# Sums over keys moved in front of the values, their additions moved behind the scores, in a fused attention and MLP kernel

## Chip, cores and metric

The kernel runs on one core of one Trainium2 chip. The metric is device time in microseconds (us) of one execution. The kernel before the change takes 1482.98 us, the median of 3 runs (1481.69 to 1483.19).

## What is computed

Attention with normalised queries and keys (8 batches, 12 heads, 448 positions, 64 features per head), followed by a two-layer MLP with the activation h - tanh(h), all in float32:

```python
q_n, k_n = rmsnorm(q, g_q), rmsnorm(k, g_k)
scores = 1/sqrt(64) * q_n @ k_n.T          # (8, 12, 448, 448)
attn = exp(scores - max); attn = attn / (sum over keys + 1e-9)
x = (attn @ v), heads side by side          # (3584, 768)
h = x @ w_in                                # (3584, 2048)
out = (h - tanh(h)) @ w_out                 # (3584, 768)
```

The weights arrive as float64 and are turned into float32 words on the chip.

## The kernel before

The work on attention is cut into 48 steps, one for each of 8 batches and 6 pairs of heads (`NP` = 6). The steps are pipelined by hand: the program of one slot `s` does the last part of step s, the scores of step s+1, transposes of step s+2, the normalising of step s+3 and the loads of step s+4. The order in which the code emits instructions is the order in each engine's queue.

The parts of a step, with their lines:

- `squares` and `norm` (L344 to L361): ScalarE squares q and k, VectorE sums the squares (L357) and scales (L359), GpSimd takes the power -1/2 (L360). `norm_q` (L363) then multiplies q on VectorE (L366), which waits for that power. `turn` (L372) transposes k and q on TensorE (L377, L381); ScalarE copies them out.
- `scores(s, half)` (L391): four matmuls (L401) with 64 rows each, two heads at a time in the two row halves of the array, give the transposed scores (keys on partitions, queries along the free axis). ScalarE takes exp straight from PSUM into the tile `p` (L406). A step has two halves, so two tiles `p` of 112 x 2 x 2 x 448.
- `add(s)` (L410): from a certain step on VectorE adds the four key chunks of `p` into one tile `sum` of 112 x 2 x 448 (one L418 and two L420). Below that step there is no addition and `sums[s]` is empty.
- `totals(s, bank)` (L435): matmuls with a matrix of ones (L443), 32 columns wide, four side by side in the array's column strips, sum over the keys. With a `sum` tile these are 4 matmuls, without one 16. VectorE takes the reciprocal from PSUM into `rs` (L448).
- `values(s, bank)` (L422): 16 matmuls (L429) of the values, also in four column strips of 32.
- `divide(s, bank)` (L450): four VectorE multiplications of the values by `rs` (L456); for the last three head pairs of a batch four more operations, on GpSimd (L469 to L472), prepare the factors of the MLP.

The profile counts two matmul instructions and two weight loads for each float32 matmul of the code.

The MLP of batch b runs during the attention of batch b+1. It is a stream (`mlp`, L687) of matmuls of 128 x 128 x 224 at L510, in a form that computes seven products instead of eight blocks (`ORDER` = 1, 5, 6, 2, 3, 7, 4). `run(ns)` (L698) takes matmuls off the stream until their planned time is used up. From slot 12 on a gap is 14 matmuls of L510, and a slot has four gaps; three slots do the first layer (`hidden`, seven products of 6 matmuls for each of four `j`), three the second (`project`, seven products of 8 matmuls for each of three `j`). The MLP of batch 0 runs in slots 6 to 11; there the second layer is written plainly (`project_first`, L675), and the weights are still being converted: ScalarE at L71 and L72, VectorE at L78, L79 and L82, GpSimd at L90, each piece behind its load.

Two pools of PSUM banks set how far TensorE can run ahead. The MLP has three banks in rotation: products 1, 5 and 6 open a bank, 2, 3 and 7 go on in those of 1, 5 and 6 once these have been read, and 4 opens the next. The readers of the first layer are L564 (ScalarE) for 1, L566 for 5, L568 for 6, L546 and L547 for 2, L576 for 3, L572 and L573 for 7, L580 for 4; all but L564 and the tanh of L546 are VectorE's. Attention has five banks `sc` in rotation: scores, transposes, totals and values take them in the order in which they are emitted.

Other tiles that matter here: `sum` and `rs` have one buffer each, `p` has three.

Slots 0 to 5 are `first_slot`; from slot 6 on it is `slot` (L743), which holds the order that is changed.

Of the kernel before, what the change touches and what calls it, by code (L numbers as in the profile page):

```python
# [92 lines left out]
def bounded_path(tc, ctx, q, k, v, moe_w_in, moe_w_out, out, g_col, ident, ones, neg_half):  # L93
# [21 lines left out]
    NP = H // 2  # L115
# [38 lines left out]
    def load(s, names):  # L154
        b, hp = steps[s]
        for name in names:
            src = {"q": q, "k": k, "v": v}[name]
            bufs = 3 if name == "v" else 2
            pair = src[b, 2 * hp : 2 * hp + 2].rearrange("h (p c) d -> p h c d", c=NCH)
            if name == "k":  # L160
                t = nat.tile([CP, NCH, 2, D], F32, name="k_nat", bufs=bufs)
                for h in range(2):
                    nc.sync.dma_start(out=t[:, :, h, :], in_=pair[:, h])
            else:
                t = nat.tile([CP, 2, NCH, D], F32, name=f"{name}_nat", bufs=bufs)
                nc.sync.dma_start(
                    out=t.rearrange("p h c d -> p h (c d)"), in_=pair.rearrange("p h c d -> p h (c d)")
                )
            loaded[name, s] = t
# [174 lines left out]
    def squares(s):  # L344
        n = nat.tile([CP, NCH, 2, D], F32, name="n", bufs=1)
        sq = nat.tile([CP, 2 * NCH, D], F32, name="sq", bufs=1), n.rearrange("p c h d -> p (c h) d")
        normed[s] = sq, n
        for i, name in ((1, "q"), (0, "k")):
            nc.scalar.activation(sq[i], loaded[name, s].rearrange("p a b d -> p (a b) d"), AF.Square)

    def norm(s):

        sq, n = normed[s]
        rr = small.tile([CP, 2, 2 * NCH], F32, name="rr", bufs=3)
        for group in ((1,), (0,)) if s < NP else ((0, 1),):
            for i in group:
                nc.vector.reduce_sum(rr[:, i], sq[i], axis=AX.X)  # L357
            r = rr[:, group[0] : group[-1] + 1].rearrange("p i r -> p (i r)")
            nc.vector.tensor_scalar(out=r, in0=r, scalar1=1.0 / D, scalar2=1e-6, op0=ALU.mult, op1=ALU.add)  # L359
            nc.gpsimd.tensor_tensor(out=r, in0=r, in1=neg_half[:, : r.shape[1]], op=ALU.pow)  # L360
        normed[s] = rr, n  # L361
# [10 lines left out]
    def turn(s, tk, tq):  # L372

        rr, n = normed.pop(s)
        kn = loaded.pop(("k", s))
        for c in range(NCH):
            nc.tensor.transpose(tk[:, c * CP : (c + 1) * CP], kn[:, c].rearrange("p h d -> p (h d)"), ident[:CP, :CP])  # L377
        kT = qkp.tile([P, S], F32, name="kT")
        nc.scalar.mul(kT, tk[:, :S], g_col)
        for c in range(NCH):  # L380
            nc.tensor.transpose(  # L381
                tq[:, c * CP : (c + 1) * CP], n[:, c].rearrange("p h d -> p (h d)"), ident[:CP, :CP]
            )
        qT = qkp.tile([P, S], F32, name="qT")
        nc.scalar.copy(out=qT, in_=tq[:, :S])
        turned[s] = rr, kT, qT

    def sc_bank():
        return ps_s.tile([P, 512], F32, name="sc")

    def scores(s, half):  # L391

        rr, kT, qT = turned[s]
        p = probs[s, half] = pp.tile([CP, 2, NCH // 2, S], F32, name="p")
        for i in range(NCH // 2):
            c = half * (NCH // 2) + i
            tiles = []
            for h in range(2):
                r = slice(h * D, (h + 1) * D)
                sc = sc_bank()  # L400
                nc.tensor.matmul(  # L401
                    sc[:CP, :S], lhsT=kT[r, c * CP : (c + 1) * CP], rhs=qT[r, :], start=True, stop=True
                )
                tiles.append(sc)
            for h in range(2):
                nc.scalar.activation(  # L406
                    p[:, h, i, :], tiles[h][:CP, :S], AF.Exp, scale=rr[:, 0, 2 * c + h : 2 * c + h + 1]
                )

    def add(s):  # L410

        if s < NP + NP // 2:
            sums[s] = []
            return
        t = sp.tile([CP, 2, S], F32, name="sum")
        sums[s] = [t]
        parts = [probs[s, c // 2][:, :, c % 2, :] for c in range(NCH)]
        nc.vector.tensor_tensor(out=t, in0=parts[0], in1=parts[1], op=ALU.add)  # L418
        for part in parts[2:]:
            nc.vector.tensor_tensor(out=t, in0=t, in1=part, op=ALU.add)  # L420

    def values(s, av):  # L422
        v_nat = loaded.pop(("v", s))
        for c in range(NCH):
            p = probs[s, c // 2]
            for m in range(2):
                for h in range(2):
                    r = (2 * m + h) * BL
                    nc.tensor.matmul(  # L429
                        av[r : r + BL, :S], lhsT=v_nat[:, h, c, m * BL : (m + 1) * BL], rhs=p[:, h, c % 2, :],  # L430
                        start=(c == 0), stop=(c == NCH - 1),
                    )
        return av

    def totals(s, dn):  # L435

        t = sums.pop(s)
        parts = t if t else [probs[s, c // 2][:, :, c % 2, :] for c in range(NCH)]
        for i, p in enumerate(parts):
            for n in range(2):  # L440
                for h in range(2):
                    r = (2 * n + h) * BL
                    nc.tensor.matmul(  # L443
                        dn[r : r + BL, :HS], lhsT=ones[:CP, :BL], rhs=p[:, h, n * HS : (n + 1) * HS],
                        start=(i == 0), stop=(i == len(parts) - 1),
                    )
        rs = whole[s] = sp.tile([P, HS], F32, name="rs")
        nc.vector.reciprocal(rs, dn[:, :HS])  # L448

    def divide(s, av):  # L450
        b, hp = steps[s]
        rs = whole.pop(s)
        x = xT[b, hp] = xp.tile([P, S], F32, name="xT")
        for n in range(2):
            for m in range(2):
                nc.vector.tensor_tensor(  # L456
                    out=x[m * D : (m + 1) * D, n * HS : (n + 1) * HS],
                    in0=av[m * D : (m + 1) * D, n * HS : (n + 1) * HS], in1=rs[n * D : (n + 1) * D], op=ALU.mult,
                )
        del probs[s, 0], probs[s, 1]  # L460
        if hp < HC:
            return
        c = hp - HC
        if c == 0:
            tt[b] = tp.tile([P, 3, HC, HS], F32, name="tt", bufs=1)
        eng = nc.vector if b == 0 and c == HC - 1 else nc.gpsimd
        x11, x12, x21, x22 = (xT[b, r][:, n : n + HS] for r in (c, hp) for n in (0, HS))
        t1, t2, t4 = (tt[b][:, i, c] for i in range(3))
        eng.tensor_tensor(out=t1, in0=x12, in1=x11, op=ALU.subtract)  # L469
        eng.tensor_tensor(out=t2, in0=x22, in1=t1, op=ALU.subtract)  # L470
        eng.tensor_tensor(out=x12, in0=x22, in1=x12, op=ALU.subtract)
        eng.tensor_tensor(out=t4, in0=x21, in1=t2, op=ALU.subtract)  # L472
# [225 lines left out]
    def run(ns):  # L698

        spent[1] += ns  # L700
        while spent[0] + 1.0 < spent[1]:
            took = next(stream, None)
            if took is None:
                return
            spent[0] += took
# [4 lines left out]
    def gap_ns(s):  # L710

        if s < 2 * NP:
            return H_NS / 12 if s % NP < 3 else 4 * S / ENGINE_NS * CD * CF / 12
        return (H_NS + O_NS) / (4 * NP)

    def has(s):
        return 0 <= s < NS
# [24 lines left out]

    def slot(s):  # L743
        gap = gap_ns(s)
        totals(s, sc_bank())
        if has(s + 1):
            scores(s + 1, 0)
        if has(s + 2):
            load(s + 2, "v")
        run(gap)  # L750
        if has(s + 2):
            turn(s + 2, sc_bank(), sc_bank())
        if has(s + 3):
            squares(s + 3)
        if has(s + 4):
            load(s + 4, "kq")
        run(gap)
        divide(s, values(s, sc_bank()))
        if has(s + 1):
            scores(s + 1, 1)  # L760
        if has(s + 3):
            norm(s + 3)
        run(gap)
        if has(s + 1):
            add(s + 1)
        if has(s + 3):
            norm_q(s + 3)
        run(gap)
# [10 lines left out]
    for s in range(NP, NS):  # L779
        slot(s)  # L780
# [319 lines left out]
```

## Time and profile before

| engine | busy us | share of the span |
|---|---|---|
| TensorE matmuls (PE) | 1442.1 | 97% |
| TensorE weight loads (PEld) | 1142.9 | 77% |
| VectorE (DVE) | 791.8 | 54% |
| ScalarE (ACT) | 469.6 | 32% |
| GpSimd (POOL) | 469.0 | 32% |

The span of the profiled execution is 1479.9 us. The page's row of slices shows TensorE at 90% or more in all but the first and the last few slices, VectorE at 80% or more in the first six (about 220 us, the conversion of the weights) and mostly at 30 to 60% after that. The granted TensorE clock is at 0.9 or more throughout.

How to read the lines: a group has its line, engine, operation, output and inputs, shapes and count, then its busy time and mean. A line of the timeline has the start in us from the span's start, the duration, the engine, the operation and its count, and in square brackets the idle time ahead of it with what ended it. The end of a matmul is modelled: consecutive matmuls overlap in the record, and distances between starts are what counts.

### The profile page before, as it was taken

What the parts mean: (1) busy time and instruction counts of PE and PEld (TensorE: products, weight loads), DVE (VectorE), ACT (ScalarE), POOL (GpSimd) and SP (SyncE); (2) the same over time, 40 slices, a digit from 0 to 9 for tenths busy, and PEclk for the clock granted to TensorE, in tenths of its full rate; (3) what the DMA queues carried; (4) which work ended last, traced back from release to release, by engine and by line L of the source; (5) the groups of instructions that cost most, each with busy time, mean ns of one, the idle gap of its engine ahead of it and who ended that gap; (6) DMA issues with size and microseconds to landing.
All of it is one profiled execution on the core that took longest, in us unless ns stands there. A gap on an engine that the chain in (4) does not pass through costs nothing.

```text
span 1479.9 us, 22097 instructions
## 1 busy us (share of the span) xinstructions
PE 1442.1 (97%) x8520; PEld 1142.9 (77%) x8520; DVE 791.8 (54%) x1165; ACT 469.6 (32%) x850; POOL 469.0 (32%) x336
## 2 busy tenths in 40 slices
PE   6889999999999999999999999999999999999997
PEld 2358744587888788878888887888788878889997
DVE  4889998656543664346534564454555356423322
ACT  6765554233222322232322233223332233200100
POOL 4556664134311343124412243212441134202310
PEclk9999999999999999999999999999999999999999
DMA  9759788854456454645465536545545654465663
GB/s 183 157 154 244 247 238 219 231 169 145 146 171 182 130 175 135 189 136 163 147 177 143 164 127 192 145 127 171 173 147 139 178 167 134 126 177 160 184 195 98
DMA packets 244997, 247.32 MB, mean 167 GB/s; under 512 B 143380, under 2 KB 187156, under 8 KB 244884
## 3 DMA queue, kind: packets, MB, share of 16 engines
q1 hardware_dynamic: 244560, 245.82, 58.0%
q8 instruction: 70, 1.15, 0.3%
q14 instruction: 43, 0.35, 0.1%
q10 hardware_dynamic: 324, 0.00, 0.0%
HBM read 212.34 MB, written 33.42 MB: 166 GB/s over the span
## 4 chain that ended last, share of the span: by engine, by line
PE 86%; DVE 10%; DMA 2%; issue 1%; SPq 0%; POOL 0%; ACT 0%; ACTq 0%; DVEq 0%; POOLq 0%
PE mm L510 60%; PE sc L401 9%; PE sc L429 9%; PE mm L675 3%; DVE sum L420 2%; PE sc L443 2%; DMA q_nat<-in_q_dram 1%; PE sc L381 1%; DVE w_out L79 1%; DVE sum L418 1%; PE sc L377 1%; DVE w_out L82 1%; DVE w_out L78 1%; DVE w_out L275 1%; DVE rr L357 1%
## 5 line engine op out<-in xcount | busy, mean ns | idle before, releaser
L406 ACT ACTIVATE p<-sc,rr 112x448 f32<-112x448 f32 x384 | 212.3, 638 | 480.2 <-PE sc L401 468.2
L510 PE MATMUL mm<-xT,w_f 128*128 128x224 f32 x1392 | 278.8, 355 | 0.0
L510 PEld LDWEIGHTS mm<-xT,w_f 128*128 128x128 f32 x1392 | 260.3, 190 | 17.3 <-issue 12.6
L510 PEld LDWEIGHTS mm<-gT,w_f 128*128 128x128 f32 x1344 | 251.3, 190 | 23.7 <-issue 23.7
L510 PE MATMUL mm<-gT,w_f 128*128 128x224 f32 x1344 | 267.8, 355 | 0.0
L360 POOL TENSOR_TENSOR rr<-rr,neg_half 112x16 f32<-112x16 f32 (+1 forms) x54 | 144.5, 2681 | 259.4 <-DVE rr L359 252.8
L510 PE MATMUL mm<-tt,w_f 128*128 128x224 f32 x1044 | 211.2, 354 | 0.0
L510 PEld LDWEIGHTS mm<-tt,w_f 128*128 128x128 f32 x1044 | 196.1, 190 | 8.0 <-issue 8.0
L510 PE MATMUL mm<-tg,w_f 128*128 128x224 f32 x1008 | 200.4, 353 | 0.0
L510 PEld LDWEIGHTS mm<-tg,w_f 128*128 128x128 f32 x1008 | 189.5, 190 | 0.0
L547 POOL TENSOR_TENSOR gT<-s,th 128x448 f32<-128x448 f32 x96 | 117.3, 1229 | 193.1 <-ACT th L546 192.4
L401 PE MATMUL sc<-qT,kT 64*112 64x448 f32 x768 | 176.3, 573 | 1.6 <-ACT p L406 1.0
L456 DVE TENSOR_TENSOR xT<-sc,rs 64x224 f32<-64x224 f32 x168 | 65.2, 388 | 140.7 <-PE sc L429 137.0
L470 POOL TENSOR_TENSOR tt<-xT,tt 128x224 f32<-128x224 f32 x23 | 15.8, 688 | 391.1 <-DVE xT L456 391.0
L401 PEld LDWEIGHTS sc<-qT,kT 64*112 64x112 f32 x768 | 63.8, 177 | 95.1 <-issue 82.4
L429 PE MATMUL sc<-p,v_nat 112*32 112x448 f32 x1344 | 135.0, 542 | 0.0
L420 DVE TENSOR_TENSOR sum<-sum,p 112x896 f32<-112x896 f32 x78 | 103.0, 1320 | 6.5 <-DVE sum L420 0.5
L429 PEld LDWEIGHTS sc<-p,v_nat 112*32 112x32 f32 x1344 | 39.4, 109 | 74.8 <-issue 73.2
L546 ACT ACTIVATE th<-s 128x448 f32<-128x448 f32 x96 | 55.3, 579 | 106.0 <-DVE s L576 47.6
L675 PE MATMUL mm<-gT,w_out 128*128 128x448 f32 x192 | 74.6, 543 | 0.4 <-POOL w_out L90 0.4
L629 DVE TENSOR_TENSOR s<-mm,s 128x224 f32<-128x224 f32 x21 | 8.2, 392 | 116.2 <-PE mm L510 116.2
L448 DVE RECIPROCAL rs<-sc 128x224 f32<-128x224 f32 x42 | 65.2, 1553 | 1.5 <-PE sc L443 1.2
(97 smaller groups left out, 1323.1 us busy)
## 6 DMA issues: line engine op xcount, KB each, us to landing
w_f<-w_in SPq DMA_DIRECT2D x196, 384.0 KB, 3.7
w_f<-w_out SPq DMA_DIRECT2D x147, 512.0 KB, 4.6
w_raw<-in_moe_w_out_dram SPq DMA_DIRECT2D x16, 768.0 KB, 5.3
k_nat<-in_k_dram SPq DMA_DIRECT2D x96, 112.0 KB, 3.4
q_nat<-in_q_dram SPq DMA_DIRECT2D x48, 224.0 KB, 4.3
v_nat<-in_v_dram SPq DMA_DIRECT2D x48, 224.0 KB, 4.8
out_dram<-th SPq DMA_DIRECT2D x192, 56.0 KB, 2.3
w_in<-w_out SPq DMA_DIRECT2D x21, 384.0 KB, 7.0
```

Of the source, the lines that this page charges most:

```text
L360: nc.gpsimd.tensor_tensor(out=r, in0=r, in1=neg_half[:, : r.shape[1]], op=ALU.pow)
L401: nc.tensor.matmul(sc[:CP, :S], lhsT=kT[r, c * CP : (c + 1) * CP], rhs=qT[r, :], start=True, stop=True)
L406: nc.scalar.activation(p[:, h, i, :], tiles[h][:CP, :S], AF.Exp, scale=rr[:, 0, 2 * c + h : 2 * c + h + 1])
L420: nc.vector.tensor_tensor(out=t, in0=t, in1=part, op=ALU.add)
L429: nc.tensor.matmul(av[r : r + BL, :S], lhsT=v_nat[:, h, c, m * BL : (m + 1) * BL], rhs=p[:, h, c % 2, :], start=(c == 0), stop=(c == NCH - 1),
L443: nc.tensor.matmul(dn[r : r + BL, :HS], lhsT=ones[:CP, :BL], rhs=p[:, h, n * HS : (n + 1) * HS], start=(i == 0), stop=(i == len(parts) - 1),)
L448: nc.vector.reciprocal(rs, dn[:, :HS])
L456: nc.vector.tensor_tensor(out=x[m * D : (m + 1) * D, n * HS : (n + 1) * HS], in0=av[m * D : (m + 1) * D, n * HS : (n + 1) * HS], in1=rs[n ...
L510: nc.tensor.matmul(bank[:, f * HS : (f + 1) * HS], lhsT=w[:, c * width + f, :], rhs=moving[p](c), start=(first and f == 0 and c == 0), sto ...
L546: nc.scalar.activation(th, h, AF.Tanh, bias=0.0, scale=1.0)
L547: eng.tensor_tensor(out=g[:, rows, cols], in0=h, in1=th, op=ALU.subtract)
L675: nc.tensor.matmul(bank[:, :S], lhsT=w_out_row(f, n // HC)[:, n % HC * P : (n % HC + 1) * P], rhs=g[:, f, :], start=(f == 0), stop=(f == C ...
```

## The change

```diff
     def add(s):
-        if s < NP + NP // 2:
+        if s <= NP + NP // 2:
             sums[s] = []
             return
...
     def slot(s):
         gap = gap_ns(s)
-        totals(s, sc_bank())
+        if s < 2 * NP:
+            totals(s, sc_bank())
         if has(s + 1):
             scores(s + 1, 0)
...
         run(gap)
+        if s >= 2 * NP:
+            totals(s, sc_bank())
         divide(s, values(s, sc_bank()))
         if has(s + 1):
             scores(s + 1, 1)
+            add(s + 1)
         if has(s + 3):
             norm(s + 3)
         run(gap)
-        if has(s + 1):
-            add(s + 1)
         if has(s + 3):
             norm_q(s + 3)
         run(gap)
```

Three edits. From slot 12 on (`2 * NP`, the third batch of attention) the sums over keys stand directly in front of the values, whose matmuls have the same shape in the array, and no longer at the head of the slot in front of the scores. In every slot from 6 on the additions of step s+1 are emitted directly behind the second half of its scores, in front of `norm` and of a gap of MLP matmuls, and no longer behind that gap. And step 9 has no additions any more: its sums take 16 matmuls over `p` instead of 4 over `sum`.

## The prediction

> **What bounds the kernel now.** I read the chain that ended last first. 86% of it is TensorE and 10% VectorE; in order of time the VectorE part lies almost wholly before 225 us, the batch 0 stage in which weights are converted. So there are two regimes, and the change touches both. Next the waits of TensorE, then timelines of single slots.
>
> The waits for the additions (columns: us in total, times, longest), first of TensorE's matmuls over the whole span, then of its weight loads from 290 us on:
>
> ```profile
> PE sc L443 <- DVE sum L420: 4.7, 3, 2.5
> ...
> PEld sc L443 <- DVE sum L420: 5.5, 12, 0.8
> PEld sc L429 <- issue: 62.8, 251, 0.3
> ```
>
> Most of the matmul wait is before 290 us; later the waits are many and small, and each weight load that opens totals or values stands 0.28 us idle anyway.
>
> The timeline of TensorE in a slot of the second regime:
>
> ```profile
> 419.53 1.68 PE L510 MATMUL mm<-gT,w_f 128*128 128x224 f32 x8
> 421.14 3.21 PE L429 MATMUL sc<-p,v_nat 112*32 112x448 f32 x32
> 424.28 1.76 PE L401 MATMUL sc<-qT,kT 64*112 64x448 f32 x8
> ...
> 433.65 3.19 PE L510 MATMUL mm<-tg,w_f 128*128 128x224 f32 x16
> 436.77 0.58 PE L443 MATMUL sc<-sum,ones 112*32 112x224 f32 x8
> 437.28 1.76 PE L401 MATMUL sc<-qT,kT 64*112 64x448 f32 x8
> ```
>
> TensorE is never without work here; what can be saved is what lies between blocks. And the end of batch 0's first layer, TensorE and then VectorE:
>
> ```profile
> 183.30 2.43 PE L510 MATMUL mm<-tt,w_out 128*128 128x224 f32 x12
> 188.28 0.89 PE L443 MATMUL sc<-sum,ones 112*32 112x224 f32 x8 [2.55 <-DVE sum L420]
> 189.10 3.10 PE L401 MATMUL sc<-qT,kT 64*112 64x448 f32 x8
> ...
> 204.08 1.77 PE L675 MATMUL mm<-gT,w_out 128*128 128x448 f32 x4 [0.38 <-POOL w_out L90]
> ...
> 224.55 0.59 PE L443 MATMUL sc<-sum,ones 112*32 112x224 f32 x8 [1.64 <-DVE sum L420]
> ```
>
> ```profile
> 183.37 1.08 DVE L418 TENSOR_TENSOR sum<-p 112x896 f32<-112x896 f32 x1
> 184.49 3.73 DVE L420 TENSOR_TENSOR sum<-sum,p 112x896 f32<-112x896 f32 x2
> 188.14 0.68 DVE L366 TENSOR_TENSOR n<-q_nat,rr 112x512 f32<-112x512 f32 x1
> ```
>
> TensorE stands before the totals of steps 9 and 10 until VectorE's additions are done.
>
> [...] a block of totals (128 x 32) keeps TensorE 0.51 us although its eight instructions are two rounds of 0.19. [...] L420 takes 1.09 us at best and 2.61 at worst, and the long ones lie beside GpSimd work. [...] At 189.10 the scores take 3.03 us to the next start instead of 1.69[...]. [...]
>
> **Part 1, the place of the totals (36 slots, 12 to 47).** Entering another mode starts the block 0.07 us before the recorded end of the block ahead: 433.65 + 3.19 against 436.77 for totals, 419.53 + 1.68 against 421.14 for values. From plain L510 straight to scores is not in the trace; the nearest is transposes to scores at 19.11, ahead of which 18.61 + 0.57 also leaves 0.07. So entering costs the same whichever block comes, and the scores take over the entry that totals paid. Totals now cost 437.28 - 436.77 = 0.51. In front of the values, in the same mode, they should cost two rounds: values' weight loads run 0.377 us per round of 448 columns, so 0.377 for two of 224. Saved: 0.51 - 0.377 = 0.135 per slot, times 36 = **4.9 us**. Bounds: 0[...], 0.2 a slot (7 us) if the entry is saved too.
>
> **Part 2, additions earlier and totals later (same slots).** The sum is now ready half a slot before its totals, so the waits of L443 go: 5.5 us less 12 x 0.28 = **2.1 us**. A second count agrees: values start at 302.95 in slot 12 and 1275.58 in slot 45, 972.63 us for 33 slots, while an undisturbed slot takes 29.41: 972.63 - 970.5 = 2.1.
>
> The reciprocal (1.55 us) moves to just before the division. VectorE waits there anyway, 137.0 us over 38 divisions; the values take 3.14 us behind the totals, so it is hidden. It now also frees the bank that the last of the four scores matmuls takes, 0.38 + 3.14 + 0.85 = 4.4 us after the totals start; the reciprocal ends some 2.2 us after. Hidden.
>
> The cost of the move: VectorE now does divide (1.63), three additions, the two reductions and a scaling (1.5) in one run, and the MLP's readings behind them wait. The second addition waits for two exps and the third for four; four exps take 2.21 us and start under the division, so with 1.09 each the additions end 3.3 us after it. In slots of the second layer they lie beside GpSimd's L469 to L472 and take up to 5; the first reading behind them (L638) is done by 432.5 and its bank is wanted at 438.97, free. In the first layer the readings stand close. The first of the three slots of a batch, now:
>
> ```profile
> 483.24 1.65 DVE L456 TENSOR_TENSOR xT<-sc,rs 64x224 f32<-64x224 f32 x4 [3.49 <-PE sc L429]
> 484.90 0.69 DVE L357 TENSOR_REDUCE rr<-sq 112x8 f32<-112x512 f32 x1
> ...
> 486.42 0.62 DVE L576 TENSOR_TENSOR s<-mm,s 128x448 f32<-128x448 f32 x1
> 488.12 0.62 DVE L572 TENSOR_TENSOR s<-mm,s 128x448 f32<-128x448 f32 x1 [1.08 <-PE mm L510]
> ```
>
> After: additions 484.9 to 488.2, norm to 489.7, L576 to 490.35. Product 1 of the next j takes L576's bank, at 490.19. A wait of 0.15 us, times 6 batches = **0.9 us lost**. L572, L573 and L580 follow by 491.95; their banks are wanted at 492.46 and 494.7. In the third slot, L568 would end at 549.5 for a bank wanted at 550.04, just free; in the second there are some 4 us. GpSimd's power (2.9) starts 3 us later and `norm_q` waits for it in VectorE's queue, with the readings L576, L557 and L566 behind; in the third slot that puts L576 at 552.5, in the trace 553.0, so nothing lost.
>
> **Part 3, step 9 without additions, step 10 with earlier ones.** Removed: VectorE from 183.37 to 188.14, 4.77 us. Added: 12 matmuls; the 32-instruction totals of an earlier slot take 153.40 to 155.05 = 1.65, so +1.14 on TensorE. TensorE could start the totals at 183.30 + 2.43 - 0.07 = 185.66, and with 1.65 + 1.69 at full clock reach L675 at 189.0 instead of 192.13. But the weights bind again at 204.08: two more pieces must come through VectorE and GpSimd. The first waits for its load (ScalarE's L71 ends at 189.9, not moved, since that load is queued behind others), takes 3.8, then L580 and the reciprocal 2.0, the second piece 3.7, L90 2.1: 201.6 instead of 204.03. Gain **2.4 us**, at most 4.1 where TensorE itself is the limit (199.9). Then at the totals of step 10: TensorE is done with L675 at 222.85 and starts at 224.55; with the additions directly behind the scores this wait of **1.7 us** is gone. The weight pieces that move behind the additions in slots 9 and 10 cost nothing: the last L90 ends at 246.28 and is used at 255.2, 9 us later.
>
> **Sum.** 4.9 + 2.1 - 0.9 + 2.4 + 1.7 = 10.2 us. 1482.98 - 10.2 = **1472.8**.
>
> **Rivals.**
> A. The mode switch isn't saved or the run of VectorE costs a few us more, and only waits go: 2.1 + 4.1 less 2 to 3, some 4 us: 1479. For it: no direct L510-to-scores in the trace, the bank margin of 0.5 us in the third slot. Against: slot 47 alone has totals to L510, also 0.52, so leaving the mode costs wherever it is done. Chance 0.17.
> B. Slower. If GpSimd slows the additions in the first layer (1.5 + 1.92 + 1.92 = 5.3 instead of 3.3 us), all readings come 2 us later: product 1 waits 2.1 in the first slot, product 7 some 1.4 in the third, 3.5 x 6 = 21 lost against 11 won: 1493. Against: GpSimd waits for the power, which VectorE issues only after the additions, and has no division work in these slots. Chance 0.08.
> C. The gains cancel: 1482, chance 0.07.
> D. More than forecast: batch 0 gains its 5.8, no stall in the first layer, a little off the entries: 4.9 + 2.1 + 5.8 + 1.5: 1468. Chance 0.13, leaving 0.55 for the forecast.
>
> **Range and chances.** 1467.5 takes in D, 1480 takes in A; B and C stay out. Faster by over 0.2% is below 1480.0: 0.85. Same 0.07, slower 0.08.
>
> **What would show it.** Values that start 29.27 us apart or less; totals to values 0.38; scores 0.07 ahead of the end of L510; no wait of L443 for L420; TensorE's L675 resuming near 201.6 and no gap before the totals of step 10. Wrong: waits of L510 for L576 or L568 beyond 1 us a batch, additions of 1.9 us in the first layer, or scores that wait for the bank of L448.

## The result, and the profile after

The changed kernel takes 1473.07 us (median, 1471.72 to 1474.74) against 1482.76 us before: a ratio of 0.9936, with a 95% interval of 0.9919 to 0.9953. That is 9.7 us less; 1472.8 had been predicted.

The page after, its row of engines and the head of the chain that ended last:

```profile
PE 1439.5 (98%) x8544; PEld 1148.3 (78%) x8544; DVE 804.7 (55%) x1162; ACT 467.4 (32%) x850; POOL 510.0 (35%) x336
...
PE 89%; DVE 6%; DMA 3%; issue 1%; POOL 0%; SPq 0%; ACT 0%; ACTq 0%; DVEq 0%; POOLq 0%
```

VectorE's share of the chain falls from 10% to 6%. Of its 150 us on the chain before, 104 lay ahead of 225 us ("almost wholly" in the prediction says too much), of its 84 us after, 42: the stage in which weights are converted hangs less on it. GpSimd is busy for 510.0 us instead of 469.0; that comes up again below.

All waits of TensorE's matmuls from 290 us on (us in total, times, longest), the only row of that answer, and the matching row of the weight loads:

```profile
PE mm L510 <- DVE s L576: 0.6, 4, 0.2
```

```profile
PEld mm L510 <- DVE s L576: 3.0, 6, 0.5
```

No totals wait for a sum any more. In their place stands the reading L576, once in each of six batches.

One slot of the second regime after, TensorE's timeline, the slot that answers to the one shown of before:

```profile
415.42 1.68 PE L510 MATMUL mm<-gT,w_f 128*128 128x224 f32 x8
417.03 0.59 PE L443 MATMUL sc<-sum,ones 112*32 112x224 f32 x8
417.43 3.19 PE L429 MATMUL sc<-p,v_nat 112*32 112x448 f32 x32
420.55 1.76 PE L401 MATMUL sc<-qT,kT 64*112 64x448 f32 x8
422.24 7.83 PE L510 MATMUL mm<-gT,w_f 128*128 128x224 f32 x40
429.91 3.19 PE L510 MATMUL mm<-tg,w_f 128*128 128x224 f32 x16
433.03 1.76 PE L401 MATMUL sc<-qT,kT 64*112 64x448 f32 x8
```

Totals and values together last from 417.03 to 420.55, 3.52 us; before, values alone took 3.14 and totals 0.51, 3.65 in all. Scores now start straight behind L510: 429.91 + 3.19 = 433.10 against 433.03, the same 0.07 us that totals had.

The end of batch 0's first layer, TensorE:

```profile
185.26 2.43 PE L510 MATMUL mm<-tt,w_out 128*128 128x224 f32 x12
187.63 1.72 PE L443 MATMUL sc<-p,ones 112*32 112x224 f32 x32
189.28 1.76 PE L401 MATMUL sc<-qT,kT 64*112 64x448 f32 x8
...
202.95 1.77 PE L675 MATMUL mm<-gT,w_out 128*128 128x448 f32 x4 [0.41 <-POOL w_out L90]
...
221.71 0.59 PE L443 MATMUL sc<-sum,ones 112*32 112x224 f32 x8
```

The totals of step 9 follow at once and without the slow matmuls of before (1.65 us to the next start, as in earlier slots; the granted clock is 1.00 from 187.60 to 190.90, where before it was 0.59 at these totals and 0.55 at the scores behind them, 188.28 to 192.13), L675 still waits for L90, and the totals of step 10 stand behind no wait. Counted from the block at 185.26 (183.30 before), L675 resumes after 17.69 us instead of 20.78 and the totals of step 10 after 36.45 instead of 41.25: 4.8 us of gain lie here. The chain that ended last now goes through the load of a piece of the weights, where it went through VectorE before:

```profile
182.63 8.51 DMA w_raw<-in_moe_w_out_dram
```

The profiled run reaches 185.26 some 2 us later than the run before reached 183.30, in code that is the same in both; the last section shows why.

### The profile page after: what moved, and what is told of

It is laid out like the page before. It is cut to its first block, busy times and chain, and to the rows that moved or that the text cites. A ratio compares the mean times of both kernels' runs of the same rounds, so it can differ in the third digit from the quotient of the medians.

```text
span 1472.3 us, 22159 instructions
## 1 busy us (share of the span) xinstructions
PE 1439.5 (98%) x8544; PEld 1148.3 (78%) x8544; DVE 804.7 (55%) x1162; ACT 467.4 (32%) x850; POOL 510.0 (35%) x336
## 4 chain that ended last, share of the span: by engine, by line
PE 89%; DVE 6%; DMA 3%; issue 1%; POOL 0%; SPq 0%; ACT 0%; ACTq 0%; DVEq 0%; POOLq 0%
PE mm L510 62%; PE sc L401 9%; PE sc L429 9%; PE mm L675 4%; PE sc L443 2%; DMA q_nat<-in_q_dram 1%; PE sc L381 1%; PE sc L377 1%; DMA w_raw<-in_moe_w_out_dram 1%; DVE sum L420 1%; DVE rr L357 1%; DVE xT L456 1%; PE mm L429 1%; DVE sum L418 0%; DMA gT<-in_moe_w_in_dram 0%
## 5 line engine op out<-in xcount | busy, mean ns | idle before, releaser
L510 PE MATMUL mm<-xT,w_f 128*128 128x224 f32 x1392 | 279.4, 355 | 0.9 <-DVE s L576 0.6
L510 PEld LDWEIGHTS mm<-xT,w_f 128*128 128x128 f32 x1392 | 259.8, 190 | 20.3 <-issue 11.3
L510 PEld LDWEIGHTS mm<-gT,w_f 128*128 128x128 f32 x1344 | 251.4, 190 | 23.4 <-issue 22.7
L510 PE MATMUL mm<-gT,w_f 128*128 128x224 f32 x1344 | 267.7, 355 | 0.0
L510 PE MATMUL mm<-tt,w_f 128*128 128x224 f32 x1044 | 211.3, 354 | 0.0
L510 PEld LDWEIGHTS mm<-tt,w_f 128*128 128x128 f32 x1044 | 196.1, 190 | 8.0 <-issue 8.0
L510 PE MATMUL mm<-tg,w_f 128*128 128x224 f32 x1008 | 200.4, 353 | 0.0
L510 PEld LDWEIGHTS mm<-tg,w_f 128*128 128x128 f32 x1008 | 189.5, 190 | 0.0
L470 POOL TENSOR_TENSOR tt<-xT,tt 128x224 f32<-128x224 f32 x23 | 32.4, 1410 | 346.8 <-DVE xT L456 346.7
L420 DVE TENSOR_TENSOR sum<-sum,p 112x896 f32<-112x896 f32 x76 | 93.8, 1235 | 7.9
L429 PEld LDWEIGHTS sc<-p,v_nat 112*32 112x32 f32 x1344 | 43.3, 111 | 70.3 <-issue 64.7
L366 DVE TENSOR_TENSOR n<-q_nat,rr 112x512 f32<-112x512 f32 x48 | 53.3, 1110 | 69.7 <-POOL rr L360 68.8
```

The lines of the kernel that those rows point to most:

```text
L366: nc.vector.tensor_tensor(out=n.rearrange("p c h d -> p h c d"), in0=t, in1=rr[:, 1].rearrange("p (h c) -> p h c", h=2)[:, :, :, None].to_ ...
L429: nc.tensor.matmul(av[r : r + BL, :S], lhsT=v_nat[:, h, c, m * BL : (m + 1) * BL], rhs=p[:, h, c % 2, :], start=(c == 0), stop=(c == NCH - 1),
L510: nc.tensor.matmul(bank[:, f * HS : (f + 1) * HS], lhsT=w[:, c * width + f, :], rhs=moving[p](c), start=(first and f == 0 and c == 0), sto ...
```

## Experiments

**1. Only step 9 without additions.**

```diff
 (kernel before)
-        if s < NP + NP // 2:
+        if s <= NP + NP // 2:
```

> Of the change only this: step 9 has no additions, 16 totals matmuls instead of 4. My theory: VectorE's chain of weights binds until the last piece of the first half, so of the 4.77 us that VectorE is rid of some 3.1 us arrive (that is how much earlier L675 resumed in the changed kernel, 20.78 us after the last first-layer block before, 17.69 after); the wait before the totals of step 10 stays. About 1479.7 us. Rival 1, the weight loads bind and nothing arrives: 1482.8. Rival 2, all arrives: 1478.

Measured 1479.65 us, ratio 0.9980 (0.9974 to 0.9987): 2.4 us below the 1482.04 of the kernel before, measured beside it, with 1.9 to 3.9 in the interval. TensorE's timeline:

```profile
183.21 2.43 PE L510 MATMUL mm<-tt,w_out 128*128 128x224 f32 x12
...
201.14 1.77 PE L675 MATMUL mm<-gT,w_out 128*128 128x448 f32 x4 [0.56 <-POOL w_out L90]
...
221.61 0.59 PE L443 MATMUL sc<-sum,ones 112*32 112x224 f32 x8 [1.65 <-DVE sum L420]
```

L675 resumes 17.93 us after the block at 183.21, 2.85 earlier than before, and the wait at step 10 stays at 1.65. So the weight chain is what binds, and of the 4.77 us taken from VectorE 2.85 arrive in the trace: VectorE's next piece (L78) has to wait for ScalarE's L71, 1.57 us, and that for its load (8.77 us from 180.58 in the chain that ended last):

```profile
190.31 0.56 DVE L78 TENSOR_SCALAR w_out<-w_out 128x768 f32<-128x768 f32 x1 [1.57 <-ACT w_out L71]
```

Both rivals, nothing and all, fall.

**2. Only the totals moved.**

```diff
 (kernel before, in slot)
-        totals(s, sc_bank())
+        if s < 2 * NP:
+            totals(s, sc_bank())
...
         run(gap)
+        if s >= 2 * NP:
+            totals(s, sc_bank())
         divide(s, values(s, sc_bank()))
```

> Of the change only this: totals in front of the values from slot 12 on, additions where they were, step 9 with additions. My theory: the array changes its mode once less per slot, 0.135 x 36 = 4.9 us, and the sums are ready when totals come, 2.1 us: 1482.8 - 7.0 = 1475.8, slots of 29.27 us in all six kinds and no wait of L510 for L576. Rival, the gain comes from the additions being early: 1481 or above.

Measured 1475.13 us, ratio 0.9958 (0.9944 to 0.9971), 6.9 us less. In the chain that ended last, values start every 29.26 to 29.28 us from slot 12 to slot 45, 29.41 to 29.95 before, and neither a sum nor L576 is waited for in these slots. The larger part of the whole gain is this edit alone, and it needs no early additions.

**3. Only the additions moved.**

```diff
 (kernel before, in slot)
             scores(s + 1, 1)
+            add(s + 1)
         if has(s + 3):
             norm(s + 3)
         run(gap)
-        if has(s + 1):
-            add(s + 1)
```

> Of the change only this: additions directly behind the scores in all slots, totals at the head of the slot everywhere, step 9 with additions. My theory: the waits go (2.1 us from slot 12 on, 1.7 at step 10, up to 2 at step 9), the wait for L576 comes (6 x 0.41 = 2.5), and the mode changes stay: 1482.8 - 3.8 - 1 + 2.5 = 1480.5, slots of 29.41 us and six of 29.8. Rival, early additions are what the change lives on: 1476 or below.

Measured 1482.11 us, ratio 1.0002 (0.9994 to 1.0011): no change that can be told from noise, where 1480.5 was expected. From slot 12 on it is as expected, 29.41 us a slot and 29.80 to 29.83 in the first slot of each batch: waits of 2.1 us go and 6 x 0.41 = 2.5 come. The miss is in batch 0. TensorE's timeline:

```profile
174.48 4.70 PE L510 MATMUL mm<-xT,w_out 128*128 128x224 f32 x24
184.35 4.37 PE L510 MATMUL mm<-xT,w_out 128*128 128x224 f32 x12 [5.17 <-DVE s L568]
188.56 2.43 PE L510 MATMUL mm<-tt,w_out 128*128 128x224 f32 x12
190.92 0.58 PE L443 MATMUL sc<-sum,ones 112*32 112x224 f32 x8
...
223.20 0.59 PE L443 MATMUL sc<-sum,ones 112*32 112x224 f32 x8
```

The early additions of step 9 stand ahead of the reading L568 in VectorE's queue. Product 7 needs its bank and waits 5.17 us instead of 1.45, and the matmuls behind that wait run slower, 4.37 instead of 2.54. The waits at the totals of steps 9 and 10 go. But nothing could be won at step 9 by moving additions that VectorE still has to do: the weight piece that L675 needs comes no earlier. GpSimd, in the kernel before and then here:

```profile
201.95 2.08 POOL L90 TENSOR_TENSOR w_out<-w_out,w_raw 128x768 int32<-128x768 int32 x1 [0.89 <-DVE w_out L82]
```

```profile
201.70 2.09 POOL L90 TENSOR_TENSOR w_out<-w_out,w_raw 128x768 int32<-128x768 int32 x1 [0.90 <-DVE w_out L82]
```

Counted from the values of slot 8 (168.31 before, 168.03 here), that piece is ready after 35.72 and 35.76 us, and the wait for L568 puts the values of slot 9 another 0.64 us later. The totals of step 10 start 1.07 us earlier than before, where I had counted on 1.7 and up to 2.

**4. Early additions in batch 0, late ones from slot 12 on.**

```diff
 (changed kernel, in slot)
             scores(s + 1, 1)
-            add(s + 1)
+            if s < 2 * NP:
+                add(s + 1)
         if has(s + 3):
             norm(s + 3)
         run(gap)
+        if s >= 2 * NP and has(s + 1):
+            add(s + 1)
```

> The changed kernel, but from slot 12 on the additions stay where they were before, behind the gap of MLP matmuls; in slots 6 to 11 they are early. My theory: totals stand half a slot later, so late additions are in time, and L576 is read before them: the 6 x 0.41 = 2.5 us of waits go, 1473.1 - 2.5 = 1470.6. Rival, totals then wait for the sum again or other readings are late: 1473 or above.

Measured 1470.50 us (1469.71 to 1472.76), ratio 0.9926 (0.9912 to 0.9939), the lowest median of all. Its interval overlaps with that of the changed kernel; the traces decide: from the values of slot 12 to those of slot 45 it takes 965.91 us, the changed kernel 968.39. The timeline of VectorE in the first slot of a batch, in the changed kernel and then here:

```profile
480.89 1.09 DVE L418 TENSOR_TENSOR sum<-p 112x896 f32<-112x896 f32 x1
482.08 2.29 DVE L420 TENSOR_TENSOR sum<-sum,p 112x896 f32<-112x896 f32 x2
...
485.80 0.62 DVE L576 TENSOR_TENSOR s<-mm,s 128x448 f32<-128x448 f32 x1
```

```profile
480.16 0.62 DVE L576 TENSOR_TENSOR s<-mm,s 128x448 f32<-128x448 f32 x1
...
484.68 1.64 DVE L418 TENSOR_TENSOR sum<-p 112x896 f32<-112x896 f32 x1
486.42 3.04 DVE L420 TENSOR_TENSOR sum<-sum,p 112x896 f32<-112x896 f32 x2
```

With the additions late, L576 is read at once, and the values follow every 29.26 to 29.28 us in all these slots. The sum is ready by 489.5; its totals come in the middle of the next slot, so it is nowhere waited for, though two additions take 3.04 us here and 2.29 there.

**5. Totals apart from the values.**

```diff
 (changed kernel, in slot)
             load(s + 2, "v")
         run(gap)
+        if s >= 2 * NP:
+            totals(s, sc_bank())
...
         run(gap)
-        if s >= 2 * NP:
-            totals(s, sc_bank())
         divide(s, values(s, sc_bank()))
```

> The changed kernel, but from slot 12 on the totals stand by themselves between MLP matmuls and the transposes, a quarter slot ahead of the values. They are as late behind the additions as a wait could ask for. My theory: the array enters and leaves its mode for them alone, 0.135 us to leave and 0.09 to enter per slot: 36 x 0.225 = 8.1 us more than the changed kernel, 1481.2, slots of 29.5 us. Rival, the place beside the values doesn't matter, only that totals no longer wait: 1473.

Measured 1483.50 us, ratio 1.0009 (1.0002 to 1.0015): 10.8 us above the changed kernel measured beside it (run 7), 2.7 more than expected. Slots take 29.55 to 29.56 us, 0.29 more instead of 0.225. TensorE's timeline:

```profile
436.92 2.43 PE L510 MATMUL mm<-tg,w_f 128*128 128x224 f32 x12
439.29 0.59 PE L443 MATMUL sc<-sum,ones 112*32 112x224 f32 x8
439.80 0.60 PE L377 MATMUL sc<-ident,k_nat 112*128 112x112 f32 x4
440.24 0.55 PE L381 MATMUL sc<-ident,n 112*128 112x112 f32 x4
```

Totals last 0.51 us again, and the first four transposes take 0.44 to the next block where they take 0.39 behind L510 in the changed kernel: the missing 0.06 (x 36 = 2). No wait appears. The same instructions in another place, with their inputs ready long before, cost 36 x 0.29 = 10.4 us: it is the neighbours that count. The rival falls.

The prices fit a simple count. Transposes follow L510 without any extra time (2.27 us from 412.70 to 414.97 before, as for twelve matmuls of L510), so only totals, values, scores and the return to L510 change the shape of the tiles: six times a slot in the kernel before (L510, totals, scores, L510, values, scores, L510), five times in the changed kernel, where totals and values are one block, and seven times here. The slots take 29.41, 29.27 and 29.55 us, some 0.14 for each change. What in a change costs that time is not shown: before, weights inside the stream of L510 are loaded 0.18 us ahead of their matmul (419.35 for 419.53), those behind a change only together with it (436.76 for 436.77); how much of the 0.14 comes from that, these runs don't tell.

**6. Step 9 with additions again.**

```diff
 (changed kernel)
-        if s <= NP + NP // 2:
+        if s < NP + NP // 2:
```

> The changed kernel, but step 9 keeps its additions (early ones, behind the scores of slot 8). My theory: VectorE's weight chain is 4.77 us longer again and some 3.1 us of it come back: 1476.2. Rival, early additions hide that chain: 1473.

Measured 1476.48 us, ratio 0.9964 (0.9951 to 0.9978): 3.8 us above the changed kernel measured beside it (1472.66, run 7), and like run 3 with a wait of 5.19 us for L568 where the changed kernel has 1.45. VectorE's timeline tells why:

```profile
178.96 1.44 DVE L418 TENSOR_TENSOR sum<-p 112x896 f32<-112x896 f32 x1
180.50 2.29 DVE L420 TENSOR_TENSOR sum<-sum,p 112x896 f32<-112x896 f32 x2
...
184.22 0.62 DVE L568 TENSOR_TENSOR s<-mm,s 128x448 f32<-128x448 f32 x1
```

L568 comes 5.3 us after the additions began. TensorE waits for this bank reading, not for the weight pieces behind the additions as was expected. But the two ways end almost together, and that the rise is near what was expected is not the bank reading's doing alone: counted from the values of slot 8, the weight piece of L675 is ready 2.95 us later than in run 7 (GpSimd's L90 ends at 204.34 here and at 200.43 there), and the values of slot 9 start 3.12 us later. By this estimate nearly the whole rise would have come without the wait for L568 too.

**7. The changed kernel again.**

> The changed kernel once more, on the same chip as the two others of this call: 1473.1 us, between 1471.5 and 1475. Its runs lay in two groups, 1472 and 1474.5; if the wait for L566 near 104 us and the clock behind it make the difference, a profile of a fast run shows 1.8 us for the eight matmuls behind that wait, one of a slow run 3.3.

Measured 1472.66 us (1471.56 to 1475.51), ratio 0.9941 (0.9928 to 0.9955). Its profile is used in the last section.

**8. Totals moved, step 9 without additions, all additions late.** This is run 2 with the edit of run 1.

> Totals in front of the values from slot 12 on and step 9 without additions, but all additions late, behind the gap, as before. It differs from the kernel with late additions from slot 12 on (1470.5 us) only in slots 9 to 11. My theory: at the totals of step 10 TensorE waits for the sum again, 1.65 us, and nothing else changes: 1472.2, and the two separate gains add up (1482.1 - 2.4 - 6.9 = 1472.8). Rival, additions early in batch 0 are worth nothing or harm: 1470.5 or below.

Measured 1472.54 us, ratio 0.9936 (0.9923 to 0.9950). The profile has the wait again:

```profile
221.19 0.59 PE L443 MATMUL sc<-sum,ones 112*32 112x224 f32 x8 [1.64 <-DVE sum L420]
```

Against run 4, which differs only in slots 9 to 11, the ratio is higher by 0.0010, 1.5 us. The intervals overlap, so the size is the trace's rather than the medians': 33.98 us from the values of slot 9 to those of slot 10, 32.28 in run 4. The gains of runs 1 and 2, 2.4 and 6.9 us, add up to the 9.1 measured here. And it equals the changed kernel within the noise: in the traces early additions gain 1.7 us in batch 0 and lose 2.5 after it.

## Why the prediction was right

Its sum was 10.2 us; 9.7 were measured, and the terms as the traces show them add up to 5.0 + 2.1 - 2.5 + 3.1 + 1.7 = 9.4. That the total came so near is in part luck: a loss set 1.6 us too small and a gain set 0.7 us too small partly cancel. By its steps:

- **The mode change, 4.9 us.** Right (mode stands for the shape of tiles that run 5 counts: 128*128 at L510, 112*32 at totals and values, 64*112 at scores). An undisturbed slot goes from 29.41 to 29.27 us, 0.14 x 36 = 5.0. Entering scores behind L510 leaves the 0.07 that was inferred from transposes ahead of scores. Totals to values take 0.40 instead of 0.38, values to scores 3.12 instead of 3.14, which cancels. Run 5 shows the opposite case, and the count there gives 0.14 for each change of shape.
- **The waits for the sum, 2.1 us.** Right: none is left from slot 12 on. But either edit does it alone: run 2 gets these 2.1 us with late additions, and in run 3 early additions remove the same waits. With the totals moved, the additions needed no moving from slot 12 on.
- **The wait for L576, 0.9 us lost.** Right in place, too small: 2.5. The first slot of a batch takes 29.68 us instead of 29.27. Product 1 starts at 486.48 where it would have started at 486.17, a wait of 0.31 instead of 0.15, and its twelve matmuls then take 2.38 us to the next start instead of 2.27: the block that restarts behind the wait pays some 0.1 (as does the one behind L568 at 182.89, 2.37), a term that the sum had not. Run 4 takes the additions out from in front of L576 and is 2.2 to 2.6 us faster by its median than the two measurements of the changed kernel, 2.5 in the traces.
- **Step 9, 2.4 us.** Right, slightly low: 3.1 in the trace of the changed kernel, 2.85 in that of run 1, and 2.4 in the measured time of run 1. The chain through the load, two weight pieces and L90 was the right one; the first piece takes 2.1 us where 3.8 were counted, the second 4.5 for 3.7. The limit of 4.1 was set too high: from 192.13 TensorE has 11.57 us of work up to the wait of 0.38 at 204.08, so from 189.0 it is ready at 200.6, not 199.9, and 3.5 us was the most that it could gain.
- **Step 10, 1.7 us.** Right: 224.55 - 204.08 = 20.47 before, 221.71 - 202.95 = 18.76 after, 1.71 less; run 8 has the wait back at 1.64.
- **What the prediction didn't see:** with early additions in slot 8, step 9's own would have moved the wait to L568 (runs 3 and 6), and would have brought the weights no earlier. The change as made leaves these additions out, so the forecast wasn't hurt; the forecast for run 3 was.

Rival B (additions slowed by GpSimd in the first layer) didn't come: two L420 take 2.29 us there, with nothing on GpSimd beside them (it is idle for 25.79 us up to 485.92). In slots of the second layer they take 2.83 beside L470 to L472, and GpSimd's times are longer too: L470 takes 1.41 us on average against 0.69 before, and L470, L471 and L472 together are busy for 98.6 us instead of 51.4; L559 and L591 are 10.6 us shorter in their place. In the kernel before, too, every L420 without GpSimd work beside it takes 1.09 us, and each of the 21 that take 1.57 us or more has some beside it. TensorE did not wait for it: from 290 us on its matmuls wait for L576 alone.

## What to carry to other kernels

Where TensorE is the bound and blocks of different tile shapes alternate, count the changes of shape and put blocks of one shape side by side; here one change less per slot was worth 0.14 us, and two more than that cost 0.29. Before an operation is moved forward in a queue, list what is behind it there and which buffer each of these frees: additions put in front of a bank reading delayed it by 3.4 us (L576) and 3.7 us (L568), counted from the division ahead of them. Test each edit of a change that wins by itself: leaving one of them out in part won 2.5 us more here.

## What the runs showed of the hardware that was not expected

TensorE does not always run slower after a wait, and the same kernel differs from run to run by that. The wait for L566 near 104 us, TensorE's timeline, in the first profile of the changed kernel and then in the profile of its second measurement:

```profile
104.65 3.35 PE L510 MATMUL mm<-xT,w_out 128*128 128x224 f32 x8 [3.09 <-DVE s L566]
107.94 4.47 PE L429 MATMUL sc<-p,v_nat 112*32 112x448 f32 x32
```

```profile
104.03 1.78 PE L510 MATMUL mm<-xT,w_out 128*128 128x224 f32 x8 [1.55 <-DVE s L566]
```

In the first, TensorE is further ahead of VectorE, waits 3.09 us, and the eight matmuls and the values behind them take 3.29 and 4.40 us to the next start instead of 1.72 and 3.14: the granted clock is 0.50 in the first of these stretches, 0.71 in the second and 1.00 behind them (112.34 to 117.00), and 2.8 us are lost. That run took 1474.11 us, the other 1471.56; whether all runs above 1474 have this cause is open, since only these two were profiled. These two waits differ in length; at the totals of step 9 they do not. In the kernel before, a wait of 2.55 us was followed by slow matmuls (0.89 us for the totals, at a granted clock of 0.59); in run 2 they took 0.59 us behind the same wait:

```profile
188.54 0.59 PE L443 MATMUL sc<-sum,ones 112*32 112x224 f32 x8 [2.55 <-DVE sum L420]
```

Behind the wait of 1.46 us for L566 in the kernel before, the granted clock was 1.00 (104.79 to 109.60). So the wait of 3.09 us was followed by slow matmuls, those of 1.46 and 1.55 were not, and one of 2.55 was in one run and not in another: the length of a wait alone does not decide here, and what does is not shown. The page's row, 0.9 or more in every slice, hides such stretches: a slice is 37 us, and they are 4 to 8 us long.
